# The second MLP's output product with the weights as the stationary operand, turned back by VectorE in 32x32 blocks

## The chip, the cores and the metric

The program runs on one core of a Trainium2 chip. The metric is the device time of one execution in microseconds (us), taken as the median of several runs. The engines are PE (TensorE: matmuls; PEld is its weight loads), DVE (VectorE), ACT (ScalarE), POOL (GpSimd) and SP, whose queue issues the DMA transfers.

## The reference

The program computes a delta-rule attention (4 batches, 8 heads, 768 positions, head size 48), whose output is 3072 tokens of 384 features, and then two MLPs one behind the other, both of 384 x 2048 x 384:

```python
x = attention(q, k, v, beta)            # (3072, 384)
h = x @ w_in; x = (P(h) / Q(h)) @ w_out     # first MLP, a rational function
h = x @ w_in2
sp = np.where(h > 20.0, h, np.log1p(np.exp(np.minimum(h, 20.0))))
out = (h * np.tanh(sp)) @ w_out2            # second MLP, Mish
```

## The kernel before

Both MLPs are cut into six token groups of 512 tokens (128 positions of each of the four batches) and sixteen slices of 128 hidden features. One group and one slice make a unit: 96 units in the first MLP, numbers 0 to 95, and 96 in the second, numbers 96 to 191. A unit has an up product (`up`, L818), the nonlinearity on its 128 x 512 tile `h`, and an output product (`down`). The product of 32-bit precision is made from operands split into a high and a low part, so each product has three terms: high by high, high by low, low by high.

The up product is 3 terms x 3 blocks of 128 input features, nine matmuls of 128 x 512 with the weights stationary and the tokens streaming. Its result has the features on the partitions. In the first MLP the output product has the same form (`Mlp1.down`, L904): nine matmuls, `lhsT` is a 128x128 block of the weights, `rhs` the 512 tokens of `gh`, three accumulators of 128 features x 512 tokens. Its result goes to a scratch tensor with features as rows, which the second MLP reads as it is.

The second MLP's output must have tokens as rows. There the output product is the other way round (`Mlp2.down`, L937): `lhsT` is a block of 128 tokens of `gh`, `rhs` all 384 output features of the weights, four accumulators (one for each batch) of 128 tokens x 384 features, so 4 x 3 = twelve matmuls of 384 columns in a unit. When the sixteenth unit of a group is done, `out_` copies each accumulator to a tile `ev` with ACT (L1022) and SP writes it to the output with one DMA (L1024).

The order on every engine is written out by hand. One turn i of the main loop issues the up product of unit i on PE, then the output product of unit i - 4, while ACT works on the Mish of unit i - 1 (`2a` L923, `2b` L928) and DVE (POOL in the first group of the second MLP) on the low part of `gh` (`2M`, L833). The accumulator's ring `o` has four banks of PSUM, `h` has two, `ev` three buffers in SBUF. The evictions of a finished group are the steps `v0` to `v3`, one behind each quarter `d0` to `d3` of the output product's list: in the first and the last unit of a group the list runs accumulator by accumulator. With 16 units to a group, the turn that ends group g is i = 96 + 16 g + 19. In the turn that is eight units ahead of a new group, SP issues the three loads of that group's tokens (`fetch_x`, L793, into the only buffer `xraw`). Three to five turns before the group starts ACT and DVE split them (`x_hi` L798, `x_lo` L802), one third in each turn. SP's queue is worked off in order, so the loads of group g + 2 stand directly behind the output DMAs of group g.

In the first group of the second MLP, DVE, ACT and POOL also convert the last eight of its weight slices (L661 to L698), each due at the up product of its unit.

Of the kernel before, what the change touches and what calls it, by code (L numbers as in the profile page):

```python
# [9 lines left out]
F32 = mybir.dt.float32  # L10
# [9 lines left out]
C = 64  # L20
GU = 2
HC = 32
TOK = 512
# [754 lines left out]
class Mlp:  # L778
# [52 lines left out]
    def lo(self, i, engine="P"):  # L831
# [2 lines left out]
            out=s["gh"][:, 1], in0=s["g"], in1=s["gh"][:, 0].bitcast(F32), op=ALU.subtract  # L834
        )

class Mlp1(Mlp):
    pool = ()

# [54 lines left out]
                out=s["g"], in0=s["q"], scalar=2.0, in1=s["r"], op0=ALU.subtract, op1=ALU.mult, reverse0=True  # L894
            )

    def down(self, i, g, f, first, last):
        def mm(j):
            def fn():
                if first and j == 0:  # L900
                    self.acc[g] = [self.ps.tile([128, TOK], F32, "o") for _ in range(3)]
                d, n = divmod(j, 3) if last or first else divmod(j, 2) if j < 6 else (j - 6, 2)
                a, b = ((0, 0), (1, 0), (0, 1))[n]
                self.nc.tensor.matmul(  # L904
                    out=self.acc[g][d], lhsT=self.w.t[f][:, a, 1, d], rhs=self.st[i]["gh"][:, b],
                    start=(first and n == 0), stop=(last and n == 2),
                )
            return fn
        return [mm(j) for j in range(9)]


class Mlp2(Mlp):


# [10 lines left out]
    def e2(self, i):  # L925
        nc, s = self.nc, self.st[i]
        s["g"] = self.sb.tile([128, TOK], F32, "g")
        nc.scalar.activation(out=s["g"], in_=s["h"], func=ACTF.Mish)  # L928

    def down(self, i, g, f, first, last):  # L930
        def mm(j):
            def fn():
                if first and j == 0:
                    self.acc[g] = [self.ps.tile([128, TOK], F32, "o") for _ in range(4)]
                t, n = divmod(j, 3) if first or last else divmod(j, 2) if j < 8 else (j - 8, 2)
                a, b = ((0, 0), (0, 1), (1, 0))[n]
                self.nc.tensor.matmul(  # L937
                    out=self.acc[g][t][:, 0:384],
                    lhsT=self.st[i]["gh"][:, a, t * 128:(t + 1) * 128],
                    rhs=self.w.t[f][:, b, 1].rearrange("p k c -> p (k c)"),  # L940
                    start=(first and n == 0), stop=(last and n == 2),
                )
            return fn
        return [mm(j) for j in range(12)]


@with_exitstack
def tile_delta_attention_two_mlps(
# [14 lines left out]
    nc = tc.nc  # L963
    B, H, S, D = q.shape
    DM = H * D
    NG = S // (GU * C)
# [22 lines left out]
    n1 = len(units)  # L989
# [15 lines left out]
    def mlp(i):  # L1005
        return m1 if i < n1 else m2

    def starts(i):
        return i == 0 or i == n1 or units[i][0] != units[i - 1][0]

    def down(i):

        g, f = units[i]
        m = mlp(i)
        last = i + 1 == n2 or starts(i + 1)

        def out_(d):
            def fn():
                acc = m.acc[g][d]
                ev = sb.tile([128, TOK], F32, "ev")  # L1020
                if i >= n1:
                    nc.scalar.copy(out=ev[:, 0:DM], in_=acc[:, 0:DM])  # L1022
                    r0 = d * S + g * GU * C
                    nc.sync.dma_start(out=out[r0:r0 + GU * C, :], in_=ev[:, 0:DM])  # L1024
                    return
                nc.scalar.copy(out=ev, in_=acc)  # L1026
                nc.sync.dma_start(out=x2[g][d * 128:(d + 1) * 128], in_=ev)
            return fn

        fns = m.down(i, g, f, starts(i), last)  # L1030
        return fns, [out_(d) for d in range(len(fns) // 3)] if last else []

    with ExitStack() as actx:
# [35 lines left out]
    with ExitStack() as bctx:  # L1069
# [22 lines left out]
        for i in range(n2 + max(LG.values())):  # L1092
# [10 lines left out]
            for op in LISTS[kind]:  # L1103
                if op in steps:
                    m, f, a = steps[op]
                    j = i - LG[op[0] + {"L": "l", "P": "l", "M": "m"}.get(op[1], op[1])]
                    if 0 <= j < n2 and mlp(j) is m:
                        f(j, *([a] if a else []))
                elif op[0] == "u" and i < n2:
                    if i not in ups:  # L1110
                        ups[i] = mlp(i).up(i, *units[i])
                    n = int(op[1])
                    run(ups[i][3 * n:3 * n + 3])
                elif op[0] in "dvy" and 0 <= i - LAG - (op[0] == "y") < n2:
                    j = i - LAG - (op[0] == "y")
                    if j not in downs:
                        downs[j] = down(j)
                    n = int(op[1])
                    if op[0] == "d":
                        run(downs[j][0][3 * n:3 * n + 3])  # L1120
                    elif (op[0] == "y") == (j < n1):
                        run(downs[j][1][n:n + 1])
                elif op == "fw" and i in fetch_w:
                    fetch, f = fetch_w[i]
                    fetch(f)
                elif op == "fx" and i + 8 < n2 and starts(i + 8):
                    mlp(i + 8).fetch_x(units[i + 8][0])
                elif op == "xa":
                    at_x(lambda m: m.x_hi)
                elif op == "xB":  # L1130
                    at_x(lambda m: lambda g, k: m.x_lo(g, k, "V"))
                elif op == "c" and i > n1:
                    w2.free = True
                    w2.word = w2.word or ps.tile([128, TOK], F32, "r")[:, 0:384]
                    conv.pull(CONV_RATE)
                elif op == "c" and i in calm:
                    conv.pull(6 * DIRECT * (calm.index(i) + 1) // len(calm) - conv.n)
                elif op == "f":
                    conv.flush()
# [29 lines left out]
```

## Time and profile before

| | |
|---|---|
| time, median of 3 runs | 1133.48 us (1131.65 to 1147.32) |
| profiled execution, its span | 1133.3 us |
| PE busy in the span | 1068.1 us (94%) |
| weight loads busy (beside PE) | 933.0 us (82%) |
| DVE / ACT / POOL busy | 720.1 / 611.6 / 538.2 us |
| second MLP's output product | 736.7 us to 1128 us |

The time of the profiled execution is its span, from the first to the last instruction; no other time lies around it in the profile. Matmuls are pipelined: a matmul's duration in a row is longer than its distance to the next one's start, so the pace of PE is read from starts, and a busy share of PE near 100% says that matmuls followed each other, not how fast.

### The profile page before, as it was taken

To read this page: it belongs to the slowest core of one execution; us is meant where nothing else is said; L and a number is where in the kernel's file an instruction comes from. 1 tells how busy PE (TensorE), PEld (TensorE's weight loads), DVE (VectorE), ACT (ScalarE), POOL (GpSimd) and SP (SyncE) were. 2 spreads that over 40 slices of the span, in tenths; PEclk is the share of its full clock that TensorE was granted. 3 is DMA by queue.
4 is the path that set the end of the run, shared out by engine and by line. 5 is a ranking of instruction groups with operands and counts; after the bars stand their busy time and mean duration, and the time that the engine had idled before them with its cause. 6 is when DMAs were issued, how large, how long until landed. Compare 5 with 4: busy or idle time off the path is not lost.

```text
span 1133.3 us, 25035 instructions
## 1 busy us (share of the span) xinstructions
PE 1068.1 (94%) x10354; PEld 933.0 (82%) x10354; DVE 720.1 (64%) x1206; ACT 611.6 (54%) x1101; POOL 538.2 (47%) x623
## 2 busy tenths in 40 slices
PE   5899899888879999999999999999999999999998
PEld 4888888778768778787887878899999998999997
DVE  5878475995669999999999999993121211212110
ACT  4415445334368888888888888743323323333322
POOL 3188878476347777787777777773000000000000
PEclk9989899988999999999999999999999999999999
DMA  7428676326585031121202036150101001010000
GB/s 139 90 54 201 163 190 172 85 59 197 178 305 204 4 108 43 50 77 52 100 17 98 14 126 249 45 190 6 56 1 56 1 1 57 1 56 1 29 1 28
DMA packets 121265, 99.23 MB, mean 88 GB/s; under 512 B 79808, under 2 KB 104512, under 8 KB 121152
## 3 DMA queue, kind: packets, MB, share of 16 engines
q1 hardware_dynamic: 120896, 97.54, 28.8%
q8 instruction: 81, 1.33, 0.5%
q14 instruction: 32, 0.26, 0.1%
q0 software_dynamic: 256, 0.10, 0.1%
HBM read 66.16 MB, written 31.46 MB: 86 GB/s over the span
## 4 chain that ended last, share of the span: by engine, by line
PE 54%; POOL 15%; ACT 11%; DVE 9%; issue 7%; DMA 2%; SPq 2%; POOLq 0%; DVEq 0%; ACTq 0%
PE h L818 21%; PE o L937 18%; POOL q L861 8%; PE o L904 4%; POOL gh L833 3%; ACT r L868 3%; POOL r L851 3%; PE y_ps L564 3%; PE c_ps L526 3%; ACT q L848 2%; ACT r L870 2%; DVE tmp L449 2%; PE c_ps L541 1%; PE c_ps L509 1%; PE s_all L549 1%
## 5 line engine op out<-in xcount | busy, mean ns | idle before, releaser
L818 PE MATMUL h<-x,w 128*128 128x512 f32 x1728 | 429.1, 393 | 7.5 <-DVE s L877 3.5
L818 PEld LDWEIGHTS h<-x,w 128*128 128x128 f32 x1728 | 321.3, 188 | 76.6 <-DVE s L877 8.7
L833 DVE TENSOR_TENSOR gh<-g,gh 128x512 fp32r<-128x512 f32 x80 | 55.4, 693 | 283.0 <-ACT g L928 274.3
L904 PE MATMUL o<-gh,w 128*128 128x512 f32 x864 | 213.5, 391 | 4.9 <-ACT ev L1026 4.9
L937 PE MATMUL o<-w,gh 128*128 128x384 f32 x1152 | 216.9, 337 | 0.0
L937 PEld LDWEIGHTS o<-w,gh 128*128 128x128 f32 x1152 | 204.7, 188 | 8.1
L904 PEld LDWEIGHTS o<-gh,w 128*128 128x128 f32 x864 | 161.7, 188 | 41.0 <-ACT ev L1026 7.8
L923 ACT ACTIVATE gh<-h 128x512 fp32r<-128x512 f32 x96 | 57.6, 600 | 229.0 <-PE h L818 229.0
L833 POOL TENSOR_TENSOR gh<-g,gh 128x512 fp32r<-128x512 f32 x112 | 145.1, 1296 | 23.9 <-ACT g L928 21.4
L861 POOL TENSOR_TENSOR q<-q,r 128x512 f32<-128x512 f32 x96 | 124.6, 1298 | 65.7 <-ACT r L855 61.2
L868 ACT ACTIVATE r<-q,cst 128x512 f32<-128x512 f32 x96 | 66.4, 691 | 52.5 <-POOL q L861 52.5
L884 DVE SCALAR_TENSOR_TENSOR q<-q,r 128x512 f32<-128x512 f32 x96 | 65.2, 679 | 15.0 <-ACT r L870 14.7
L698 POOL TENSOR_TENSOR w<-wm,w 128x384 fp32r<-128x384 f32 x48 | 49.6, 1035 | 52.6 <-ACT w L693 52.4
L857 ACT ACTIVATE s<-h,ab 128x512 f32<-128x512 f32 x96 | 74.3, 774 | 0.0
L877 DVE SCALAR_TENSOR_TENSOR s<-s,ab,h 128x512 f32<-128x512 f32 x96 | 71.8, 748 | 3.4
L888 DVE SCALAR_TENSOR_TENSOR r<-s,ab,r 128x512 f32<-128x512 f32 x96 | 71.7, 746 | 0.0
L875 DVE TENSOR_TENSOR s<-s,h 128x512 f32<-128x512 f32 x96 | 65.4, 681 | 6.0 <-ACT s L857 6.0
L893 DVE SCALAR_TENSOR_TENSOR g<-q,r 128x512 f32<-128x512 f32 x96 | 65.9, 687 | 3.3
L455 POOL TENSOR_TENSOR xs<-xs,tmp 128x30 f32<-128x30 f32 (+14 forms) x120 | 62.1, 518 | 9.4
L449 POOL TENSOR_TENSOR tmp<-xs 128x30 f32<-128x30 f32 (+14 forms) x120 | 58.3, 486 | 7.0
L829 ACT CAST gh<-g 128x512 fp32r<-128x512 f32 x96 | 59.7, 622 | 0.0
L851 POOL TENSOR_SCALAR r<-q,ab 128x512 f32<-128x512 f32 x54 | 42.1, 780 | 34.8 <-ACT q L848 34.8
(125 smaller groups left out, 1397.0 us busy)
## 6 DMA issues: line engine op xcount, KB each, us to landing
w<-w SPq DMA_DIRECT2D x36, 768.0 KB, 7.3
w<-in_moe_w_in_dram SPq DMA_DIRECT2D x32, 384.0 KB, 4.0
w<-in_moe_w_out_dram SPq DMA_DIRECT2D x32, 384.0 KB, 3.4
xraw<-x SPq DMA_DIRECT2D x36, 256.0 KB, 3.9
w<-wt SPq DMA_DIRECT2D x8, 768.0 KB, 3.8
kn<-in_k_dram SPq DMA_DIRECT2D x48, 96.0 KB, 3.7
qn<-in_q_dram SPq DMA_DIRECT2D x48, 96.0 KB, 3.4
v<-in_v_dram SPq DMA_DIRECT2D x48, 96.0 KB, 3.5
```

What stands on the lines that cost most here:

```text
L449: eng.tensor_tensor(out=tv, in0=ls[:, j, j + 1:HC].unsqueeze(1).to_broadcast([128, j, n]), in1=xs[:, 0:j, j:j + 1].to_broadcast([128, j, n ...
L818: self.nc.tensor.matmul(out=self.st[i]["h"], lhsT=self.w.t[f][:, a, 0, k], rhs=self.x[g][:, b, k], start=(n == 0), stop=(n == 8),)
L833: (nc.gpsimd if engine == "P" else nc.vector).tensor_tensor(out=s["gh"][:, 1], in0=s["g"], in1=s["gh"][:, 0].bitcast(F32), op=ALU.subtract)
L851: nc.gpsimd.tensor_scalar(out=s["r"], in0=s["q"], scalar1=k["b1"], scalar2=k["b0"], op0=ALU.mult, op1=ALU.add)
L857: nc.scalar.activation(out=s["s"], in_=s["h"], func=ACTF.Identity, scale=k["a3"], bias=k["a2"])
L861: nc.gpsimd.tensor_tensor(out=s["q"], in0=s["q"], in1=s["r"], op=ALU.mult)
L868: nc.scalar.activation(out=s["r"], in_=s["q"], func=ACTF.Ln, bias=k["c"])
L877: nc.vector.scalar_tensor_tensor(out=s["s"], in0=s["s"], scalar=k["a1"], in1=s["h"], op0=ALU.add, op1=ALU.mult)
L888: nc.vector.scalar_tensor_tensor(out=s["r"], in0=s["s"], scalar=k["a0"], in1=s["r"], op0=ALU.add, op1=ALU.mult)
L893: nc.vector.scalar_tensor_tensor(out=s["g"], in0=s["q"], scalar=2.0, in1=s["r"], op0=ALU.subtract, op1=ALU.mult, reverse0=True)
L904: self.nc.tensor.matmul(out=self.acc[g][d], lhsT=self.w.t[f][:, a, 1, d], rhs=self.st[i]["gh"][:, b], start=(first and n == 0), stop=(last ...
L937: self.nc.tensor.matmul(out=self.acc[g][t][:, 0:384], lhsT=self.st[i]["gh"][:, a, t * 128:(t + 1) * 128], rhs=self.w.t[f][:, b, 1].rearran ...
```

## The change

The form of the output product becomes a property of the token group. `down` (weights stationary, 512 tokens streaming, nine matmuls in a unit, three accumulators) moves to the base class and is used by the second MLP for its groups 0 to 4. The old form, now `down_rows`, stays for the last group. For groups 0 to 4 an accumulator now has 128 features on the partitions and 512 tokens in the row, so `out_` turns it: DVE transposes it in blocks of 32x32 from PSUM into `ev`. After that each block holds 32 tokens on the partitions and 32 features in the row, but a block stands where its mirror image should. The DMAs put the blocks in their places: for each accumulator 4 strips of 32 partitions x 4 batches, 16 DMAs of 16 KB, each with 128 runs of 128 bytes in the output. A group ends with 3 DVE transposes and 48 DMAs, where it had 4 ACT copies and 4 DMAs. The last group is evicted as before.

```diff
--- before.py
+++ after.py
@@ -834,6 +834,37 @@
             out=s["gh"][:, 1], in0=s["g"], in1=s["gh"][:, 0].bitcast(F32), op=ALU.subtract
         )
 
+    def down(self, i, g, f, first, last):
+        def mm(j):
+            def fn():
+                if first and j == 0:
+                    self.acc[g] = [self.ps.tile([128, TOK], F32, "o") for _ in range(3)]
+                d, n = divmod(j, 3) if last or first else divmod(j, 2) if j < 6 else (j - 6, 2)
+                a, b = ((0, 0), (1, 0), (0, 1))[n]
+                self.nc.tensor.matmul(
+                    out=self.acc[g][d], lhsT=self.w.t[f][:, a, 1, d], rhs=self.st[i]["gh"][:, b],
+                    start=(first and n == 0), stop=(last and n == 2),
+                )
+            return fn
+        return [mm(j) for j in range(9)]
+
+    def down_rows(self, i, g, f, first, last):
+        def mm(j):
+            def fn():
+                if first and j == 0:
+                    self.acc[g] = [self.ps.tile([128, TOK], F32, "o") for _ in range(4)]
+                t, n = divmod(j, 3) if first or last else divmod(j, 2) if j < 8 else (j - 8, 2)
+                a, b = ((0, 0), (0, 1), (1, 0))[n]
+                self.nc.tensor.matmul(
+                    out=self.acc[g][t][:, 0:384],
+                    lhsT=self.st[i]["gh"][:, a, t * 128:(t + 1) * 128],
+                    rhs=self.w.t[f][:, b, 1].rearrange("p k c -> p (k c)"),
+                    start=(first and n == 0), stop=(last and n == 2),
+                )
+            return fn
+        return [mm(j) for j in range(12)]
+
+
 class Mlp1(Mlp):
     pool = ()
 
@@ -894,21 +925,6 @@
                 out=s["g"], in0=s["q"], scalar=2.0, in1=s["r"], op0=ALU.subtract, op1=ALU.mult, reverse0=True
             )
 
-    def down(self, i, g, f, first, last):
-        def mm(j):
-            def fn():
-                if first and j == 0:
-                    self.acc[g] = [self.ps.tile([128, TOK], F32, "o") for _ in range(3)]
-                d, n = divmod(j, 3) if last or first else divmod(j, 2) if j < 6 else (j - 6, 2)
-                a, b = ((0, 0), (1, 0), (0, 1))[n]
-                self.nc.tensor.matmul(
-                    out=self.acc[g][d], lhsT=self.w.t[f][:, a, 1, d], rhs=self.st[i]["gh"][:, b],
-                    start=(first and n == 0), stop=(last and n == 2),
-                )
-            return fn
-        return [mm(j) for j in range(9)]
-
-
 class Mlp2(Mlp):
 
 
@@ -926,23 +942,6 @@
         nc, s = self.nc, self.st[i]
         s["g"] = self.sb.tile([128, TOK], F32, "g")
         nc.scalar.activation(out=s["g"], in_=s["h"], func=ACTF.Mish)
-
-    def down(self, i, g, f, first, last):
-        def mm(j):
-            def fn():
-                if first and j == 0:
-                    self.acc[g] = [self.ps.tile([128, TOK], F32, "o") for _ in range(4)]
-                t, n = divmod(j, 3) if first or last else divmod(j, 2) if j < 8 else (j - 8, 2)
-                a, b = ((0, 0), (0, 1), (1, 0))[n]
-                self.nc.tensor.matmul(
-                    out=self.acc[g][t][:, 0:384],
-                    lhsT=self.st[i]["gh"][:, a, t * 128:(t + 1) * 128],
-                    rhs=self.w.t[f][:, b, 1].rearrange("p k c -> p (k c)"),
-                    start=(first and n == 0), stop=(last and n == 2),
-                )
-            return fn
-        return [mm(j) for j in range(12)]
-
 
 @with_exitstack
 def tile_delta_attention_two_mlps(
@@ -1018,6 +1017,16 @@
             def fn():
                 acc = m.acc[g][d]
                 ev = sb.tile([128, TOK], F32, "ev")
+                if i >= n1 and g < NG - 1:
+                    nc.vector.transpose(out=ev, in_=acc)
+                    for r in range(4):
+                        for t in range(B):
+                            r0 = t * S + g * GU * C
+                            nc.sync.dma_start(
+                                out=out[r0:r0 + GU * C, d * 128 + 32 * r:d * 128 + 32 * r + 32].rearrange("(b r) c -> r b c", r=32),
+                                in_=ev[32 * r:32 * r + 32, t * GU * C:(t + 1) * GU * C].rearrange("r (b c) -> r b c", c=32),
+                            )
+                    return
                 if i >= n1:
                     nc.scalar.copy(out=ev[:, 0:DM], in_=acc[:, 0:DM])
                     r0 = d * S + g * GU * C
@@ -1027,7 +1036,7 @@
                 nc.sync.dma_start(out=x2[g][d * 128:(d + 1) * 128], in_=ev)
             return fn
 
-        fns = m.down(i, g, f, starts(i), last)
+        fns = (m.down_rows if i >= n1 and g == NG - 1 else m.down)(i, g, f, starts(i), last)
         return fns, [out_(d) for d in range(len(fns) // 3)] if last else []
 
     with ExitStack() as actx:
```

## Rows read from the trace of the kernel before

**Rows 1.** The page: the span, and busy time by engine (share of the span, instructions)

```profile
span 1133.3 us, 25035 instructions
...
PE 1068.1 (94%) x10354; PEld 933.0 (82%) x10354; DVE 720.1 (64%) x1206; ACT 611.6 (54%) x1101; POOL 538.2 (47%) x623
```

**Rows 2.** The page: the span in 40 slices (busy tenths of DVE; granted TensorE clock)

```profile
DVE  5878475995669999999999999993121211212110
...
PEclk9989899988999999999999999999999999999999
```

**Rows 3.** The chain of waits from 700 us on, shares by line

```profile
by line: PE h L818 47.4%; PE o L937 45.5%; PE o L904 4.1%; DMA out_dram<-ev 0.4%; ACT ev L1022 0.2%; issue 0.0%; ACTq L1022 0.0%
```

**Rows 4.** Table by stage: busy time in one token group of the second MLP

```profile
core 0: us, PE busy (x) PEld busy (x) DVE busy (x) ACT busy (x) POOL busy (x), PEclk, DMA share, GB/s
...
800.20:867.20 67.00, 67.00 (x338) 60.74 (x337) 12.88 (x19) 20.63 (x40) 0.00 (x0) 1.00 0.07 24
```

**Rows 5.** Timeline of PE, second MLP: start us, us, engine, line, operation, count

```profile
830.89 2.24 PE L818 MATMUL h<-x,w 128*128 128x512 f32 x9
...
851.83 2.24 PE L818 MATMUL h<-x,w 128*128 128x512 f32 x9
...
853.91 2.27 PE L937 MATMUL o<-w,gh 128*128 128x384 f32 x12
...
876.95 2.24 PE L818 MATMUL h<-x,w 128*128 128x512 f32 x9
```

**Rows 6.** Timeline of PE, first MLP, a stretch without waits

```profile
479.94 2.20 PE L818 MATMUL h<-x,w 128*128 128x512 f32 x9
...
500.33 2.20 PE L818 MATMUL h<-x,w 128*128 128x512 f32 x9
```

**Rows 7.** Timeline of PE where the second MLP's output product begins

```profile
734.64 2.20 PE L818 MATMUL h<-x,w 128*128 128x512 f32 x9
...
736.68 2.27 PE L937 MATMUL o<-w,gh 128*128 128x384 f32 x12
...
738.79 2.24 PE L818 MATMUL h<-x,w 128*128 128x512 f32 x9
```

**Rows 8.** Groups by line: form, count | busy us, mean ns | idle before, releaser

```profile
L1022 ACT COPY ev<-o 128x384 f32<-128x384 f32 x24 | 11.5, 480 | 34.9 <-PE o L937 25.9 <-DMA out_dram<-ev 8.4
...
L462 DVE STREAM_TRANSPOSE xt<-xs 128x1024 f32<-128x1024 f32 x5 | 10.4, 2090 | 0.0
...
L462 DVE STREAM_TRANSPOSE xt<-s_all 128x1024 f32<-128x1024 f32 x1 | 1.9, 1900 | 0.0
```

**Rows 9.** Timeline of SP's queue at the first group boundary of the second MLP

```profile
800.71 2.83 SPq L1024 DMA_DIRECT2D out_dram<-ev  x4
...
803.59 1.40 SPq L793 DMA_DIRECT2D xraw<-x  x3
```

**Rows 10.** Issue time of single lines: ns min/median/max, first and last start

```profile
L1024 SPq DMA_DIRECT2D out_dram<-ev x24: 332/333/1611, 800.7 to 1130.0; - x24
...
L653 SPq DMA_DIRECT2D w<-in_moe_w_in_dram x32: 378/384/893, 21.5 to 760.2; - x32
...
L238 SPq DMA_DIRECT2D kn<-in_k_dram x48: 595/633/1754, 0.8 to 192.1; - x48
```

**Rows 11.** The page: DMA issues (KB each, median us from issue to landing)

```profile
xraw<-x SPq DMA_DIRECT2D x36, 256.0 KB, 3.9
```

**Rows 12.** Table by stage, two short stretches with DMA at work

```profile
12.90:18.90 6.00, 5.93 (x40) 5.69 (x39) 0.49 (x3) 1.31 (x5) 0.00 (x0) 1.00 0.75 118
...
1128.20:1131.00 2.80, 0.36 (x3) 0.04 (x1) 0.00 (x0) 0.83 (x2) 0.00 (x0) 1.00 0.64 229
```

**Rows 13.** Timeline of ACT when the next group's tokens are split

```profile
829.96 0.63 ACT L798 CAST x<-xraw 128x512 fp32r<-128x512 f32 x1
...
833.17 0.60 ACT L923 ACTIVATE gh<-h 128x512 fp32r<-128x512 f32 x1 [2.59 <-PE h L818]
```

**Rows 14.** Timeline of POOL: the last converted weights of the second MLP

```profile
772.79 2.44 POOL L698 TENSOR_TENSOR w<-wm,w 128x384 fp32r<-128x384 f32 x2
```

## The prediction

> **What bounds the kernel now.** I read the page first. PE is busy for 94% of the span, nothing else for more than 82%, and that 82% is PE's own weight loads [rows 1]. The slices then show that the second MLP, the last fourteen of the 40, is a stage with its own balance: DVE is full until slice 27 (the conversion of the last weights) and nearly idle after that, and the granted clock is full [rows 2]. The chain of waits from 700 us on settles what sets the end there: it consists of the up product and the output product, 47.4% and 45.5%, and of almost nothing else; ACT's evictions have 0.2% [rows 3]. The table by stage says the same of one token group: PE 67.00 us busy of 67.00, ACT 20.63, DVE 12.88, POOL nothing, granted clock 1.00, which is the 2.4 GHz level [rows 4]. So in this stage only PE's pace counts. Work that moves from ACT to DVE moves between two engines with room, and it costs nothing unless it makes PE wait.
>
> A busy share does not tell PE's pace, so I take it from starts. In the second MLP the up product of one unit starts at 851.83 us and that of the sixth unit after it at 876.95 us: 25.12 / 6 = 4.187 us for a unit of nine matmuls of 512 columns and twelve of 384 [rows 5]. In the first MLP, in a stretch where PE waits for nobody, five units take 500.33 - 479.94 = 20.39 us, 4.078 us for a unit of eighteen matmuls of 512 columns [rows 6]. Both units stream the same number of columns: 9 x 512 + 12 x 384 = 18 x 512 = 9216. The first MLP's unit is the instruction stream that the change gives to the second MLP, with the same operand types and the same clock, so the price of the new form stands in the trace of before.
>
> **The output product, part one of the change.** In 80 of the second MLP's units (groups 0 to 4) twelve matmuls of 384 columns give way to nine of 512. The difference of the two paces is 4.187 - 4.078 = 0.109 us in a unit, 80 x 0.109 = 8.7 us. Where it lies: 512 columns at 2.4 GHz are 213.3 ns, and the first MLP needs 4078 / 18 = 226.6 ns for each, so 13.3 ns are spent per matmul beside its columns. In the second MLP the up product takes 853.91 - 851.83 = 2.08 us, which leaves 4.187 - 2.08 = 2.107 us for the twelve, 175.6 ns each against 160 ns for the columns, so 15.6 ns beside them. The output product alone therefore saves 2.107 - 2.04 = 0.067 us in a unit. The remaining 0.04 us are in the up product: each of the nine up matmuls takes (853.91 - 851.83) / 9 = 231 ns in this stage [rows 5], not 226.6. That is not a property of the second MLP's weights or tokens: before its output product begins, the same up product on the same token group takes 736.68 - 734.64 = 2.04 us (226.7 ns each), and the first one behind the twelve matmuls of 384 columns starts the slower kind [rows 7]. I therefore expect it to go when the 384-column matmuls go. If it stays, the sum is smaller; that is a rival below.
>
> The Trainium skill's page "TensorE: Matmul & The Clock Gate", section "Back-to-back issue gap", speaks against the change: a matmul with N columns at the full clock costs N / 2.4 ns and only about 2.5 ns more. By it, three matmuls less would save 3 x 2.5 ns x 80 = 0.6 us, as an estimate from that page, where the rows give 8.7 us. The traces of this case do not agree with it at these sizes: they show 13.3 and 15.6 ns beside the columns.
>
> **Operands.** The stationary operand was `gh`, fresh from ACT and DVE, and becomes the weights, which lie ready; `gh` streams instead. It is still needed four turns after its up product, so the wait neither comes nor goes. One accumulator less in a ring of four frees a bank: the first accumulator of the next group finds a bank that nobody reads, and the ones behind it are free after the transposes.
>
> **The eviction.** Removed: 20 ACT copies of 0.48 us and 20 output DMAs. They were not on the chain [rows 3, 8], so nothing is gained. Added: 15 DVE transposes of 128x512. The trace has this operation only at 128x1024: 2.09 us from SBUF, 1.90 us in the one instance whose source is in PSUM [rows 8]. Half the columns bound it between half of that, 0.95 us, and the full 2.1 us; I take 1.0. Three of them in a group are 3 to 6 us of DVE time, in a stage where DVE has 67.00 - 12.88 = 54 us free [rows 4]. Behind them on DVE stand only low parts of `gh`, which are needed three turns (12 us) later. In group 0 the transposes come after the conversion, whose last weights are made at 772.79 + 2.44 = 775.2 us [rows 14]; their up product (unit 111, eleven units behind the one at 734.64) is due at 734.64 + 11 x 4.078 = 779.5 us in the new pace instead of 780.7 us, so 4 us of cover remain. Cost: nothing.
>
> **The 48 DMAs of a boundary.** This is the one place where the change can lose. They go through SP, and directly behind them stand the loads of the group after next; today SP issues four output DMAs from 800.71 us on and the loads at 803.59 us [rows 9]. One DMA's issue takes 0.333 us in the present output, 0.384 us for a load in pieces of 1 KB, and 0.633 us for a four-way pattern with 512 pieces of 192 bytes [rows 10]. The new ones have 128 pieces in a three-way pattern, nearest to the second; I take 0.40, with 0.33 and 0.63 as ends. Transfer: each of the 16 DMA engines gets 48 x 128 / 16 = 384 packets of 128 bytes. With 192-byte reads they moved 118 GB/s at a busy share of 0.75, which is 0.75 x 16 x 192 / 118 = 19.5 ns for a packet; with the present output's 1536-byte writes 0.64 x 16 x 1536 / 229 = 69 ns [rows 12]. So a boundary's packets take between 7.5 and 26.5 us, and by either end SP's issue, 16 to 30 us, is the longer of the two or nearly equal.
>
> Now the deadline. Counted from the end of the first accumulator (800.2 us in the trace: SP's first issue less ACT's 0.48 us copy), the loads are issued after 1.0 + 48 x 0.40 = 20.2 us and have landed 0.4 + 3.9 us later [rows 11], at 24.5 us. ACT's first split stands at 829.96 us [rows 13], 29.8 us after that end, 29.0 in the new pace. So they arrive 4.5 us early. With 0.633 us an issue they land at 35.7 us, 6.7 us late. ACT would stand there with the next Mish behind the split. But PE has two `h` banks: the up product two units after the one at 830.89 us [rows 5] begins at 839.3 us, and only then must that unit's Mish (1.1 us, after a split of 0.63 us) be done, so the split may begin as late as 837.5 us, 7.5 us after its place. Even 0.633 us is just covered; the limit is at 0.65 us for each DMA, issue or transfer. No cost.
>
> **Sum.** 1133.3 us, which is both the span and the whole of the profiled execution's time, less 8.7 us gives 1124.6 us. The median of the runs is 1133.48 us, 0.2 us above it, so the forecast is 1124.8 us, rounded 1125.
>
> **The rivals.** *The pace does not improve that much.* For it: I infer from one transition that the 384-column matmuls disturb the up product, and no row shows the second MLP's output product in the new form. If the up product stays at 2.08 us and the new output product takes 2.04, a unit saves 4.187 - 4.12 = 0.067 us, 5.4 us in all: 1128.1 us. If both take 2.08, it saves 0.027 us, 2.2 us in all: 1131.3. If only columns counted, nothing: 1133.5. Against it stand the five even units of the first MLP. *The loads come late (slower).* Place: ACT's split before groups 2 to 5, four times. From 0.65 us for each DMA on, every further 0.1 us holds PE up for 4.8 us at a boundary, 19 us in all. The gain is gone at 0.65 + 8.7 / 192 = 0.695 us; 2% slower, 1156 us, needs 0.81; at 1.0 us the time would be 1124.8 + 4 x 48 x 0.35 = 1192 us. For it: no row shows 128-byte writes to DRAM, and a small write may cost more than a small read. Against it: 0.81 us for each DMA means 101 ns for a packet, more than the 69 ns of a packet twelve times its size.
>
> The Trainium skill's page "DMA: Bandwidth & Descriptors", section "Specifications", gives this rival its mechanism: below 512 bytes a DMA engine reads, modifies and writes. No row here shows that on a write.
>
> **How the numbers follow.** The forecast gets 0.70, the smaller gain 0.17 (1128 to 1133.5), late loads 0.11, something faster that I do not see 0.02. The range 1121 to 1137 takes in the forecast with the spread of undisturbed runs (1131.65 against 1133.48 before), the whole of the smaller gain, and late loads up to 0.71 us for each DMA; about one in ten is left out. About 2% is what a measurement of this kernel can tell from no change. A gain over 2% (under 1111) has no mechanism here: 0.02. Slower by over 2% is the part of the late loads beyond 0.81 us: 0.06. Within 2%: 0.92.
>
> **What would show it.** In the new trace starts of successive up products in groups 0 to 4 should be 4.08 us apart and those of the last group 4.19; nine output matmuls should take 2.04 us, and the up product should fall from 2.08 to 2.04 too. DVE's transposes should take 1.0 us. SP's loads should be issued some 20 us after the first output DMA of a boundary, and ACT's split should wait for no DMA. Waits of PE for a Mish five to seven units behind each boundary would prove the second rival; an up product still at 2.08 us would prove the first.

## The result

The changed kernel takes 1126.17 us, the median of 6 runs (1117.91 to 1138.52), beside 1136.36 us before (1131.65 to 1147.32, 6 runs). The ratio is 0.9889 with a 95% interval of 0.9842 to 0.9935: about 1% faster, within 2%, and clear of no change. The ratio leaves out one run of the changed kernel (1138.52 us), which fell in a slower state with a lower granted clock (0.960, the others 0.976 to 0.980). In twelve further runs it is 0.9911 (0.9879 to 0.9943). The forecast was 1125 us, within 2%.

The page of the changed kernel: the span (1133.3 us before), and busy time by engine, to set beside [rows 1].

```profile
span 1122.8 us, 24782 instructions
...
PE 1059.6 (94%) x10114; PEld 900.0 (80%) x10114; DVE 727.8 (65%) x1221; ACT 602.5 (54%) x1081; POOL 538.9 (48%) x623
```

PE has 240 matmuls fewer, 3 in each of 80 units, and is as full as before. The timeline of PE in a group of the second MLP, changed kernel (start us, us, engine, line, operation, count; L844 is the output product in its new form), answers to [rows 5]:

```profile
851.40 2.20 PE L818 MATMUL h<-x,w 128*128 128x512 f32 x9
853.45 2.20 PE L844 MATMUL o<-gh,w 128*128 128x512 f32 x9
855.49 2.20 PE L818 MATMUL h<-x,w 128*128 128x512 f32 x9
...
875.88 2.20 PE L818 MATMUL h<-x,w 128*128 128x512 f32 x9
```

Six units take 875.88 - 851.40 = 24.48 us, 4.080 us each, where they took 4.187 us [rows 5]. The up product, which the change does not touch, starts 853.45 - 851.40 = 2.05 us ahead of the output product, and that one 2.04 us ahead of the next. Same view, where the stage begins and where the last group, in its old form (L858), takes over:

```profile
735.12 2.20 PE L844 MATMUL o<-gh,w 128*128 128x512 f32 x9
...
1059.48 2.20 PE L818 MATMUL h<-x,w 128*128 128x512 f32 x9
1061.53 2.27 PE L858 MATMUL o<-w,gh 128*128 128x384 f32 x12
1063.63 2.24 PE L818 MATMUL h<-x,w 128*128 128x512 f32 x9
1065.71 2.27 PE L858 MATMUL o<-w,gh 128*128 128x384 f32 x12
```

The 80 units of groups 0 to 4 take 1061.53 - 735.12 = 326.41 us. Before, the same stretch began at 736.68 us [rows 7] and ended with this start of the last group's first output product:

```profile
1071.91 2.27 PE L937 MATMUL o<-w,gh 128*128 128x384 f32 x12
```

That is 1071.91 - 736.68 = 335.23 us, so the stage gained 8.8 us. The spans differ by 10.5 us. Of the rest, 1.6 us lie ahead of the stage, in code that the change leaves alone: the stretch began at 735.12 instead of 736.68 us. As soon as the last group's twelve matmuls of 384 columns are back, the up product is back at its old pace, 1065.71 - 1063.63 = 2.08 us, in the same execution on the same weights.

The boundaries, changed kernel. SP's queue (48 output DMAs, then the loads of the group after next), DVE's transposes, and ACT's first split of the next tokens, each from its engine's timeline:

```profile
797.95 23.63 SPq L1025 DMA_DIRECT2D out_dram<-ev  x48
821.67 1.32 SPq L793 DMA_DIRECT2D xraw<-x  x3
```

```profile
797.21 0.72 DVE L1021 STREAM_TRANSPOSE ev<-o 128x512 f32<-128x512 f32 x1 [7.03 <-PE o L844]
797.85 0.65 DVE L833 TENSOR_TENSOR gh<-g,gh 128x512 fp32r<-128x512 f32 x1
798.41 1.31 DVE L1021 STREAM_TRANSPOSE ev<-o 128x512 f32<-128x512 f32 x2
```

```profile
826.06 0.62 ACT L798 CAST x<-xraw 128x512 fp32r<-128x512 f32 x1
```

The row of the split names no DMA as what it waited for. The table by stage for the 65.3 us from this boundary to the next (columns as in [rows 4]) shows PE without a gap:

```profile
797.20:862.50 65.30, 65.30 (x289) 54.05 (x288) 14.60 (x23) 18.94 (x36) 0.00 (x0) 1.00 0.12 25
```

So the turn and the 48 DMAs are hidden. What stays open after the result is where the 0.107 us of a unit come from. Three matmuls less is one answer. The prediction took part of it from the pace of the up product, on the strength of one transition. And the limit of 0.65 us for each DMA was only argued.

### The profile page after: what moved, and what is told of

Read it like the earlier page. It is cut to its first block, busy times and chain, and to the rows that moved or that the text cites. A ratio compares the mean times of both kernels' runs of the same rounds, so it can differ in the third digit from the quotient of the medians.

```text
span 1122.8 us, 24782 instructions
## 1 busy us (share of the span) xinstructions
PE 1059.6 (94%) x10114; PEld 900.0 (80%) x10114; DVE 727.8 (65%) x1221; ACT 602.5 (54%) x1081; POOL 538.9 (48%) x623
## 4 chain that ended last, share of the span: by engine, by line
PE 53%; POOL 15%; ACT 11%; DVE 8%; issue 6%; DMA 4%; SPq 1%; POOLq 0%; DVEq 0%; ACTq 0%
PE h L818 21%; PE o L844 18%; POOL q L892 8%; POOL gh L833 3%; ACT r L899 3%; POOL r L882 3%; PE o L858 3%; PE y_ps L564 2%; ACT q L879 2%; ACT r L901 2%; PE c_ps L526 2%; DMA w<-in_moe_w_out_dram 2%; DVE tmp L449 2%; PE c_ps L509 2%; DMA w<-in_moe_w_in_dram 1%
## 5 line engine op out<-in xcount | busy, mean ns | idle before, releaser
L844 PE MATMUL o<-gh,w 128*128 128x512 f32 x1584 | 389.6, 390 | 5.0 <-ACT ev L1035 5.0
L818 PEld LDWEIGHTS h<-x,w 128*128 128x128 f32 x1728 | 322.1, 188 | 80.7 <-DVE s L908 12.9
L844 PEld LDWEIGHTS o<-gh,w 128*128 128x128 f32 x1584 | 296.8, 188 | 69.3 <-ACT ev L1035 7.9
L939 ACT ACTIVATE gh<-h 128x512 fp32r<-128x512 f32 x96 | 57.5, 599 | 253.9 <-PE h L818 253.9
L879 ACT ACTIVATE q<-h 128x512 f32<-128x512 f32 x96 | 57.2, 595 | 1.9 <-PE h L818 1.9
L901 ACT ACTIVATE r<-r 128x512 f32<-128x512 f32 x96 | 55.9, 582 | 3.1
```

The lines of the kernel that those rows point to most:

```text
L818: self.nc.tensor.matmul(out=self.st[i]["h"], lhsT=self.w.t[f][:, a, 0, k], rhs=self.x[g][:, b, k], start=(n == 0), stop=(n == 8),)
L844: self.nc.tensor.matmul(out=self.acc[g][d], lhsT=self.w.t[f][:, a, 1, d], rhs=self.st[i]["gh"][:, b], start=(first and n == 0), stop=(last ...
L879: nc.scalar.activation(out=s["q"], in_=s["h"], func=ACTF.Abs)
L901: nc.scalar.activation(out=s["r"], in_=s["r"], func=ACTF.Exp, scale=-1.0)
```

## The experiments

**Which property of the old form slows the up product?** The old form differs from the up product in three ways: 384 columns instead of 512, `gh` instead of the weights as stationary operand, twelve matmuls instead of nine. Theory M says that two lengths side by side are what costs; theory S that it is the stationary operand, or the count. Three kernels take the properties apart. Each ran once and is read from starts in its own trace, not from its time. The first keeps the new form and shortens it to 384 columns (here and below `...` stands for lines of the edit that are left out):

```diff
-                    out=self.acc[g][d], lhsT=self.w.t[f][:, a, 1, d], rhs=self.st[i]["gh"][:, b],
+                    out=self.acc[g][d][:, 0:self.cols], lhsT=self.w.t[f][:, a, 1, d],
+                    rhs=self.st[i]["gh"][:, b, 0:self.cols],
...
 class Mlp2(Mlp):
+    cols = 384
```

> The changed kernel, but in groups 0 to 4 of the second MLP the output product streams 384 of the 512 tokens (weights stationary, nine matmuls of 384 columns; the last 128 tokens of each group are left out, and batch 3 is written from batch 0's tokens). Theory M, two matmul lengths side by side slow both: the up product takes 2.08 us as before the change, the output product 9 x 175.5 = 1.58 us, 3.66 us for a unit. Theory S, it was gh as the stationary operand (or the twelve in place of nine) that slowed the up product: up 2.04 us, output 9 x 173.3 = 1.56 us, 3.60 us for a unit.

Timeline of PE, the new form at 384 columns (L846):

```profile
861.38 2.24 PE L818 MATMUL h<-x,w 128*128 128x512 f32 x9
863.47 1.75 PE L846 MATMUL o<-gh,w 128*128 128x384 f32 x9
865.05 2.24 PE L818 MATMUL h<-x,w 128*128 128x512 f32 x9
...
868.72 2.24 PE L818 MATMUL h<-x,w 128*128 128x512 f32 x9
```

The up product takes 2.09 us, the output product 1.58, a unit (868.72 - 861.38) / 2 = 3.67 us: theory M's numbers. Neither the stationary operand nor the count of twelve is needed for the slow pace.

The second kernel keeps the old form, `gh` stationary and twelve matmuls, and lengthens it to 512 columns:

```diff
+                n_cols, at = (512, 1024 if b else 384) if g < 5 else (384, 768 * b + 384)
...
-                    out=self.acc[g][t][:, 0:384],
+                    out=self.acc[g][t][:, 0:n_cols],
...
-                    rhs=self.w.t[f][:, b, 1].rearrange("p k c -> p (k c)"),
+                    rhs=self.w.t[f].rearrange("p a s k c -> p (a s k c)")[:, at:at + n_cols],
```

> The old form of the output product in all groups (gh stationary, twelve matmuls, ACT evicts, four DMAs), but in groups 0 to 4 each matmul streams 512 columns in place of 384 (128 columns of other weights ride along, their sums are not read, and the high part's 512 columns begin at the right place while the low part's begin 128 early, so the values are not the reference's). Theory M, two lengths side by side: all matmuls are alike, so up 2.04 us, output 12 x 226.7 = 2.72 us, 4.76 us for a unit. Theory S, gh as the stationary operand: up stays at 2.08 us, output above 2.72 us (12 x 231 = 2.77).

```profile
862.84 2.88 PE L859 MATMUL o<-w,gh 128*128 128x512 f32 x12
865.56 2.20 PE L818 MATMUL h<-x,w 128*128 128x512 f32 x9
867.60 2.88 PE L859 MATMUL o<-w,gh 128*128 128x512 f32 x12
```

In the timeline of PE the output product (L859) takes 865.56 - 862.84 = 2.72 us, 226.7 ns a matmul, and the up product 2.04 us. With all lengths alike the old operands run at full pace. The third kernel makes all matmuls of the second MLP 384 columns long, with Mish and the low parts cut alike:

```diff
-                    out=self.st[i]["h"], lhsT=self.w.t[f][:, a, 0, k], rhs=self.x[g][:, b, k],
+                    out=self.st[i]["h"][:, 0:self.cols], lhsT=self.w.t[f][:, a, 0, k],
+                    rhs=self.x[g][:, b, k, 0:self.cols],
...
 class Mlp2(Mlp):
+    cols = 384
```

> The changed kernel, but every matmul of the second MLP, up and output, streams 384 of the 512 tokens, in all six groups (128 tokens of each group are left out, batch 3 is written from batch 0's tokens; the last group is turned too). Read in groups 1 to 4, since group 0 waits for its weights' conversion. Theory M: all alike, 18 x 173.3 = 3.12 us for a unit. Rival L, 384 columns are too short to cover a weight load, whatever stands beside them: 18 x 175.5 = 3.16 us or more, with uneven distances.

```profile
859.90 1.72 PE L818 MATMUL h<-x,w 128*128 128x384 f32 x9
861.46 1.72 PE L848 MATMUL o<-gh,w 128*128 128x384 f32 x9
...
869.26 1.72 PE L818 MATMUL h<-x,w 128*128 128x384 f32 x9
```

Six products take 869.26 - 859.90 = 9.36 us, 173.3 ns a matmul. So a weight load is covered by 384 columns too, and rival L falls. At either length, among its like, a matmul costs 13.3 ns beside its columns (226.7 - 213.3, 173.3 - 160).

**How long does the slow pace last?** In the kernel before, each up product of the second MLP is done twice over, which makes the runs of 512 columns twice as long:

```diff
-        return [mm(n) for n in range(9)]
+        return [mm(n) for n in range(9 * self.passes)]
...
 class Mlp2(Mlp):
+    passes = 2
```

> The kernel before, with each up product of the second MLP done twice over (eighteen matmuls of 512 columns in a row, the second nine begin the sum anew and give the same values), beside the twelve of 384 columns. Theory T, the slow pace is a transient after each change of matmul length: the first nine take 2.08 us, the second nine 2.04, the twelve 2.107 as before, 6.23 us for a unit. Rival C, the pace stays low as long as both lengths alternate, whatever the length of a run: both nines take 2.08 us, 6.27 us.

Timeline of PE (here the up product is L819, the old output product L939). The second row is from a view that opens inside the run of eighteen, and begins at its tenth matmul:

```profile
865.68 4.28 PE L819 MATMUL h<-x,w 128*128 128x512 f32 x18
867.76 2.20 PE L819 MATMUL h<-x,w 128*128 128x512 f32 x9
869.80 2.27 PE L939 MATMUL o<-w,gh 128*128 128x384 f32 x12
871.90 4.28 PE L819 MATMUL h<-x,w 128*128 128x512 f32 x18
```

The first nine matmuls take 867.76 - 865.68 = 2.08 us, the second nine 869.80 - 867.76 = 2.04 us: theory T. A unit takes 6.22 us. The slow pace is a transient that follows a change of length. Against 18 x 226.7 = 4.08 us the run of 512 columns loses 0.04 us; the twelve of 384 columns take 871.90 - 869.80 = 2.10 us against 12 x 173.3 = 2.08, a loss of some 0.02 to 0.03. How long the transient lasts in the run of 384 columns, the kernel before shows, in a view that opens at the seventh of the twelve matmuls that begin at 853.91 us [rows 5]:

```profile
854.97 1.20 PE L937 MATMUL o<-w,gh 128*128 128x384 f32 x6
856.01 0.39 PE L818 MATMUL h<-x,w 128*128 128x512 f32 x1
```

The first six take 854.97 - 853.91 = 1.06 us, the last six 856.01 - 854.97 = 1.04 us, which is 6 x 173.3. So the disturbance is over after six matmuls of 384 columns, and after nine of 512. What the array does in them no run here shows.

**Where is the limit for the boundary's DMAs?** Each output DMA is cut into two, so that SP issues 96:

```diff
-                                in_=ev[32 * r:32 * r + 32, t * GU * C:(t + 1) * GU * C].rearrange("r (b c) -> r b c", c=32),
...
+                            for k in range(2):
+                                p = 32 * r + 16 * k
+                                nc.sync.dma_start(
+                                    out=o[16 * k:16 * k + 16],
+                                    in_=ev[p:p + 16, t * GU * C:(t + 1) * GU * C].rearrange("r (b c) -> r b c", c=32),
```

> The changed kernel with each of the 48 output DMAs of a boundary cut into two of 64 runs: the same packets, twice the issues. If SP's issue is what takes the 23.6 us of a boundary, 96 x 0.45 = 43 us; the next tokens then land 0.7 + 43 + 0.4 + 3.8 = 48 us after the first accumulator's end, 11.5 us past the limit of 36.5 us that the prediction put, and PE is held for about 11 us at four boundaries: 46 us longer in all. If it is the packets, 24 us for a boundary as before and no wait: no change from the changed kernel.

This kernel's span is 1195.9 us. From its timelines of SP (first, second and last group that is turned), ACT and PE (first boundary):

```profile
805.45 45.77 SPq L1028 DMA_DIRECT2D out_dram<-ev  x96
851.32 1.32 SPq L793 DMA_DIRECT2D xraw<-x  x3
...
886.40 45.98 SPq L1028 DMA_DIRECT2D out_dram<-ev  x96
...
1131.84 46.69 SPq L1028 DMA_DIRECT2D out_dram<-ev  x96
```

```profile
853.99 0.62 ACT L798 CAST x<-xraw 128x512 fp32r<-128x512 f32 x1 [20.32 <-DMA xraw<-x]
```

```profile
855.65 4.21 PE L818 MATMUL h<-x,w 128*128 128x512 f32 x9 [12.90 <-ACT g L944]
859.65 2.84 PE L844 MATMUL o<-gh,w 128*128 128x512 f32 x9
862.33 2.21 PE L818 MATMUL h<-x,w 128*128 128x512 f32 x9
```

The issues are what takes the time: half the runs in each, twice the DMAs, 45.8 us instead of 23.6. ACT's split waits 20.3 us for its tokens and PE waits 12.9 us, so 7.4 us of lateness were covered. The boundary costs more than that wait, though: from one boundary's first DMA to the next it is 886.40 - 805.45 = 80.95 us, against 65.28 us (sixteen units of 4.08), 15.7 us more. The rest is the clock. The table by stage, this kernel (the third number from the end is the granted clock):

```profile
843.00:855.60 12.60, 0.00 (x0) 0.00 (x0) 0.69 (x1) 1.61 (x4) 0.00 (x0) 0.67 0.29 75
855.60:858.60 3.00, 2.95 (x7) 2.38 (x8) 2.59 (x4) 2.00 (x4) 0.00 (x0) 0.50 0.00 0
858.60:862.30 3.70, 3.70 (x12) 2.88 (x12) 0.69 (x1) 1.08 (x2) 0.00 (x0) 0.69 0.00 0
862.30:886.40 24.10, 24.10 (x108) 19.93 (x107) 3.51 (x6) 6.52 (x12) 0.00 (x0) 1.00 0.00 1
```

While PE waited the granted clock fell (0.67 in the mean of the first row), and PE restarted at 0.50, the 1.2 GHz level. The first up product took 859.65 - 855.65 = 4.00 us and the output product 2.68, 2.6 us more than at the full clock: 12.9 + 2.6 = 15.5. The expectation had 11.5 us for a boundary: the wait itself is 1.4 us longer, and the clock, which it did not count, adds 2.6. All four boundaries together cost 1131.84 - 805.45 - 4 x 65.28 = 65.3 us, where the expectation had 46.

**Why the last group keeps its form.** All six groups are turned:

```diff
-                if i >= n1 and g < NG - 1:
+                if i >= n1:
...
-        fns = (m.down_rows if i >= n1 and g == NG - 1 else m.down)(i, g, f, starts(i), last)
+        fns = m.down(i, g, f, starts(i), last)
```

> The changed kernel with the last group turned as well: its output product runs in the new form and its end is 3 DVE transposes and 48 DMAs. Theory: PE gains 16 x 0.109 = 1.7 us, and the end, now 6.2 us from the first accumulator's end to the span's end, becomes 0.8 + 48 x 0.49 + 1.5 = 25.8 us, since nothing runs beside it: about 18 us longer than the changed kernel. Rival, the DMAs of an idle chip go faster than those beside a running PE: at 0.33 us each the end is 18 us and the kernel 10 us longer.

Timelines of DVE and SP, end of this kernel, whose span is 1136.2 us:

```profile
1110.30 2.08 DVE L1021 STREAM_TRANSPOSE ev<-o 128x512 f32<-128x512 f32 x3 [7.03 <-PE o L844]
...
1111.05 22.61 SPq L1025 DMA_DIRECT2D out_dram<-ev  x48
```

From the transposes to the end of the span it is 25.9 us (25.8 expected). In the changed kernel the last group's ACT copies begin at this row:

```profile
1116.64 1.52 ACT L1031 COPY ev<-o 128x384 f32<-128x384 f32 x3 [7.78 <-PE o L858]
```

That leaves 6.2 us to the end of its span. From the first up product (315.3 us in the changed kernel, 310.2 us here) to the end the two take 807.5 and 826.0 us, so the turn of the last group costs 18.5 us (about 18 expected). Beside an idle PE SP needs 22.61 / 48 = 0.47 us for a DMA, hardly less than the 0.49 us beside a running one and far from the rival's 0.33.

**The changed kernel again**, with no edit, twelve executions beside sixteen of the kernel before:

> The changed kernel once more, in five rounds beside the kernel before. The stage's own saving is 8.8 us of about 1135 us: ratio 0.992. If the earlier stages also gained, as the first comparison's 0.9889 could be read, 0.989.

The ratio is 0.9911 (0.9879 to 0.9943). The interval holds both 0.992 and 0.989, so it does not tell them apart; the stage's 8.8 us are known from starts in single traces, not from this. These runs add a second trace of the changed kernel, of an execution that took 1137.43 us:

```profile
747.91 1.30 PE L844 MATMUL o<-gh,w 128*128 128x512 f32 x5
...
1074.31 1.92 PE L858 MATMUL o<-w,gh 128*128 128x384 f32 x10
```

The 80 units take 1074.31 - 747.91 = 326.40 us again, where the first trace had 326.41. The new stage repeats to the hundredth of a microsecond while the whole time does not; of the kernel before there is one trace.

## Why the prediction was right, step by step

- **PE's pace as the only thing that counts.** Right: PE is busy for 65.30 of 65.30 us across a boundary, and the stage's gain of 8.8 us is the pace (80 x 0.107 = 8.6 us) and a remainder of some 0.3 us that the trace before has over its pace (335.23 - 80 x 4.187). The remainder was not forecast. It lies in a single unit of that trace, behind the third boundary, which takes 942.13 - 937.64 = 4.49 us. There the fourth ACT copy waited for an output DMA, the Mish behind it was late (it ended at 939.90 us), and the up product that needs its bank began at 939.95 us, 0.2 us late. So the old eviction did hold PE once, where the prediction had "nothing is gained"; that this wait is the cause is read from the rows, no run tests it. From the timelines of ACT and PE, kernel before:

```profile
938.43 0.48 ACT L1022 COPY ev<-o 128x384 f32<-128x384 f32 x1 [2.71 <-DMA out_dram<-ev]
```

```profile
939.95 2.34 PE L818 MATMUL h<-x,w 128*128 128x512 f32 x9
```

- **The price taken from the first MLP's stretch.** Right: 4.080 us where [rows 6] gave 4.078.
- **How it splits.** The sum was right and one term mis-sized. The prediction gave the old output product 15.6 ns for each matmul beside its columns, as if it were a cost of every matmul. The uniform kernels show 13.3 ns at both lengths. Three matmuls less are therefore 3 x 13.3 = 0.040 us of the unit's 0.107. The larger part, 0.067 us, is the change of length: 0.04 in the up product and 0.027 (2.107 - 2.08) in the twelve. The guess that the 384-column matmuls disturb the up product was shown right by the new form shortened to 384 columns and by the old one lengthened to 512. The rival in which the up product stays slow is out: 2.04 to 2.05 us.
- **The rule against the change.** By the Trainium skill's page "TensorE: Matmul & The Clock Gate", section "Back-to-back issue gap", 2.5 ns per matmul, which the section gives as the gap of an isolated matmul, would have left a gain of 0.6 us, as an estimate. The traces do not agree: here a matmul has 13.3 ns beside its columns, and the transient after a change of length comes on top.
- **The eviction.** Hidden, as said. A transpose of 128x512 from PSUM takes 0.70 us, below both bounds (0.95 and 2.1 us): half the columns take much less than half of the 1.90 us in [rows 8]. The bound from half the time was therefore wrong; it cost nothing, since DVE had room.
- **The DMAs of a boundary.** Covered, as said, with three terms mis-sized. SP needs 23.63 / 48 = 0.49 us for each, where 0.40 was taken, between the two ends. The transpose takes 0.7 us, where 1.0 was taken. The first of the three loads, which is all that the first split reads, lands 2.7 us after its issue begins, where 0.4 + 3.9 us was taken from the median of all loads. The view of the DMA issues, changed kernel, 821.60 to 822.05 us:

```profile
xraw<-x SPq DMA_DIRECT2D x1, 256.0 KB, 2.7
```

The load issued at 821.67 us is there at 824.4, some 1.7 us ahead of the split at 826.06, where 4.5 us were forecast. Of the limit's two parts the second is confirmed by the 96 DMAs: 7.4 us of lateness covered, 7.5 said. With both parts as measured the limit is, as an estimate, 0.49 + (1.7 + 7.4) / 48 = 0.68 us for each DMA, beside the 0.65 of the prediction. Transfer did not set the time: 128-byte writes cost no more than the reads of [rows 12]. Between 799 and 820 us, by the table by stage below, they took 0.22 x 16 x 128 / 34 = 13 ns a packet. The Trainium skill's page "DMA: Bandwidth & Descriptors", section "Specifications", has writes below 512 bytes read and modified first; if they are here, it costs nothing that this row shows.

```profile
799.00:820.00 21.00, 21.00 (x94) 17.38 (x94) 4.75 (x8) 5.43 (x10) 0.00 (x0) 1.00 0.22 34
```

- **The price of a late load**, in the slower rival, was too low: it counted the wait alone. The 96 DMAs show 2.6 us more at the first boundary, from the clock.
- **The time around the span.** The prediction took the span as the whole of the execution's time and found the median 0.2 us above it. The changed kernel's profiled execution took 1124.55 us with a span of 1122.8: 1.75 us lie around it. If as much lay around the span of the kernel before, the sum is 1133.3 + 1.75 - 8.7 = 1126.4 us, nearer to the measured 1126.17 than the forecast's 1125. Since the stretches ahead of the second MLP vary by more from one execution to the next, that closeness proves little.

## What to carry to other kernels

Read PE's pace from the starts of successive products, not from its busy share: 94% stood on the page of both kernels. Where two products alternate on a full PE, give them the same column count: here that was worth more than the matmuls saved. A turn by VectorE with many small DMAs behind it is free as long as the queue's next load still lands in time, and it belongs nowhere near the end of the program, where it cost 18.5 us here; count issues, not bytes.

## What the runs showed of the hardware

- After a change between 384 and 512 columns, PE's pace is uneven, for nine matmuls in a run of 512 columns and for six in a run of 384. It costs some 0.04 us in a run of 512 columns and some 0.027 us in a run of 384, whichever operand is stationary, with the granted clock at 1.00 throughout.
- Executions differ ahead of the MLPs. The first up product starts at 317.1 us in the trace before, at 315.3 and 326.9 in the two of the changed kernel and at 310.2 in the one with all groups turned, though the code up to there is the same. These differences are as large as the change's whole effect, so the effect had to be read from the stage itself. The lines of the up product, before, changed, and changed again:

```profile
L818 PE MATMUL h<-x,w x1728: 386/390/505, 317.1 to 1117.7; 128*128 128x512 f32 x192
```

```profile
L818 PE MATMUL h<-x,w x1728: 387/389/504, 315.3 to 1107.3; 128*128 128x512 f32 x192
```

```profile
L818 PE MATMUL h<-x,w x1728: 387/389/628, 326.9 to 1120.1; 128*128 128x512 f32 x192
```

- A DVE transpose of 128x512 takes 0.70 us with its source in PSUM, one of 128x1024 1.90 us (a single instance, [rows 8]).
- A DMA of 16 KB in runs of 128 bytes lands 1.5 us after its issue (median of 240), sooner than the 2.0 us of the last group's 192 KB ones.
